# Attention feeding a gated MLP: the second stage begins two steps earlier, three weight pieces are converted beside it, and five smaller edits

## The chip, the cores and the metric

One NeuronCore of a Trainium2 chip runs the whole program. The metric is the device time of one execution in microseconds; smaller is better. The kernel before took 519.78 us (median of three runs, 519.24 to 522.22).

## What is computed

Float32 attention over 4 batches, 8 heads, 576 positions and head size 64, with rotary positions on q and k, feeds a small MLP with a convolution over positions in its gate. Cut to what matters:

```python
q_rot, k_rot = (rotate(q), rotate(k))
scores = 1.0 / np.sqrt(D) * np.matmul(q_rot, k_rot.transpose(0, 1, 3, 2))
attn = softmax(scores)                                # rows of 576
x = np.matmul(attn, v)  -> (B, S, H * D)              # 4 x 576 x 512
h = np.maximum(x @ w_in, 0.0)                         # 512 -> 1024
conv_out = sum over k of conv_w[k] * hp[:, k:k + S, :]    # 3 taps along S
out = h * sigmoid(conv_out) @ w_out                   # 1024 -> 512
```

`w_in`, `conv_w` and `w_out` arrive as 64-bit floats and are turned into 32-bit ones on the chip.

## The kernel before

**Pairs and steps.** Two heads make a pair, so there are 16 pairs (`p`), four to a batch. Each pair takes five steps (`s` 0 to 4): four of 128 queries for each of its two heads, and a last one with the 64 remaining queries of both. Step n = 5p + s. The order of all work is written by hand: `at(n, rank, fn)` puts a piece of work into step n, a smaller rank earlier, and every engine executes its own share in the order in which it was issued. `defer(k, fn)` puts work k ticks later, where a tick passes with about every group of products on TensorE.

**Attention of a step.** S (`emit_S`, line 245) makes the scores, VectorE takes the negated row maximum (`soft`, line 260), ScalarE the exponential with its row sum (line 264). T (`emit_T`, line 305) turns the probabilities on TensorE in 64-wide pieces, and ScalarE copies them into `pt` (line 189). The remainder turns (`emit_Trem`, line 333) do the last 64 keys; their copy is ScalarE's in the first stage and VectorE's (line 191) in the second. E (`emit_E`, line 362) multiplies the turned probabilities by v, once for each half (290 positions) of the sequence; `emit_rinv` sends the reciprocal sums through DRAM, and `norm` (line 380) and `split` (line 384) divide and store the result as a high and a low part in `xT`, the low part by GpSimd (line 387).

**Before the products.** The queue of SyncE loads q and k of a pair in 32-wide blocks; GpSimd rotates them (`rope`, lines 180 and 183), VectorE turns them in 32 x 32 blocks (`emit_TQ`, lines 224 and 228), and five ticks later ScalarE multiplies the turned q by the scale in place (line 225). `krem` (line 232) is a block-diagonal copy of the last 64 keys of both heads, used in the first stage.

**Two stages.** Up to step `WIDE` = 26 ("wide") only attention runs, with score tiles of three PSUM banks; S is issued a step ahead, and one product with `krem` (line 276) serves the last keys of both heads before the two wide ones (lines 280, 281). Beside it all 16 weight pieces (128 x 512, `conv_w_piece`, line 538) are converted: ScalarE line 497, VectorE lines 500, 506, 509 and 514, ScalarE line 557, GpSimd line 560 four times. From step 26 on ("narrow") the score tiles have two banks and two buffers, S is issued in its own step (a tile for each head, one tile for the last queries, made by four products of 64 x 64, lines 299 and 300), and the MLP runs between the attention products.

**The MLP.** Block `blk` is half a batch (288 positions). M1 (`emit_M1`, line 391) is 12 products for one of 8 feature groups; ScalarE takes the ReLU (409), then follow `conv` (VectorE, 413 and 415 twice, 2 ticks later), `tanh` (ScalarE, 421, 5 ticks), `gate` (VectorE, 424, 7 ticks) and `split` (ScalarE 432 and GpSimd 433, 9 ticks). M2 (`emit_M2`, line 469) is six products, a quarter of a 128-position tile of the output. Six blocks are spread over ten steps each from step `WIDE` on, by the weights `room` (line 666): 0.35 for a step with n % 5 of 0 or 1, which hold the E products (line 653), and 1.0 for the others. The last two blocks follow in a tail without attention.

## Time and profile before

| | |
|---|---|
| median of three runs | 519.78 us |
| the profiled execution's own time | 519.74 us |
| its span, first to last instruction | 518.0 us |
| busy: TensorE (PE) | 477.5 us, 92% of the span |
| busy: VectorE (DVE), ScalarE (ACT), GpSimd (POOL) | 370.4, 318.8, 300.4 us |
| mean granted TensorE clock | 0.974 of full speed |

The span and the execution's own time differ by 1.74 us, which lies around the span. TensorE is an in-order engine here: where it is busy all the time, work added to it or taken from it changes the time one for one, and where it waits, the engine it waits for decides. A window row gives its stretch, its length, the busy time (and instructions) of PE, of PE's weight loads, of DVE, ACT and POOL, then PEclk, the share of DMA and GB/s. "busy" of a stretch is read beside the length of the stretch; PEclk is the mean granted clock of that stretch, where 1.00 stands for 2.4 GHz and 0.50 for 1.2 GHz. In the rows `x8` counts instructions, and a float32 product is two of them. A bracket at the end of a row is the idle time before the instruction and what ended it.

### The profile page before, as it was taken

To read this page: it belongs to the slowest core of one execution; us is meant where nothing else is said; L and a number is where in the kernel's file an instruction comes from. 1 tells how busy PE (TensorE), PEld (TensorE's weight loads), DVE (VectorE), ACT (ScalarE), POOL (GpSimd) and SP (SyncE) were. 2 spreads that over 40 slices of the span, in tenths; PEclk is the share of its full clock that TensorE was granted. 3 is DMA by queue.
4 is the path that set the end of the run, shared out by engine and by line. 5 is a ranking of instruction groups with operands and counts; after the bars stand their busy time and mean duration, and the time that the engine had idled before them with its cause. 6 is when DMAs were issued, how large, how long until landed. Compare 5 with 4: busy or idle time off the path is not lost.

```text
span 518.0 us, 10786 instructions
## 1 busy us (share of the span) xinstructions
PE 477.5 (92%) x3880; PEld 350.1 (68%) x3880; DVE 370.4 (72%) x656; ACT 318.8 (62%) x836; POOL 300.4 (58%) x479
## 2 busy tenths in 40 slices
PE   2779789897999899999999999999999998999997
PEld 1346455563777477776867677767767676889986
DVE  5788988996597758694877578674867464748951
ACT  2678778886677566666666666674575554325520
POOL 3799978999585827665574838390482121314530
PEclk9979987997999899999999999999999999999999
DMA  8986664943424243434333341513320201000011
GB/s 225 174 165 152 160 145 137 212 98 69 93 47 93 48 91 68 93 68 92 68 73 66 87 74 44 105 52 83 59 67 1 66 2 45 21 22 22 0 42 61
DMA packets 139257, 42.61 MB, mean 82 GB/s; under 512 B 132012, under 2 KB 132804, under 8 KB 139204
## 3 DMA queue, kind: packets, MB, share of 16 engines
q1 hardware_dynamic: 137860, 41.54, 36.2%
q8 instruction: 30, 0.49, 0.4%
q10 hardware_dynamic: 1344, 0.39, 0.3%
q14 instruction: 23, 0.19, 0.1%
HBM read 37.12 MB, written 4.79 MB: 81 GB/s over the span
## 4 chain that ended last, share of the span: by engine, by line
PE 71%; DVE 10%; ACT 8%; SPq 3%; DMA 3%; issue 2%; POOL 2%; DVEq 0%; ACTq 0%; POOLq 0%
PE pm L401 13%; PE sp L252 13%; PE tp L368 13%; PE pm L479 11%; PE mt L479 8%; PE tp L312 6%; PE mt L401 5%; DVE negm L260 3%; ACT st L264 3%; ACT pt L189 3%; SPq L140 1%; DVE c L415 1%; PE sp L368 1%; DMA rq<-q 1%; DVE wt L506 1%
## 5 line engine op out<-in xcount | busy, mean ns | idle before, releaser
L260 DVE TENSOR_REDUCE negm<-sp 128x1 f32<-128x576 f32 x144 | 102.4, 747 | 57.2 <-PE sp L252 55.1
L189 ACT ACTIVATE pt<-tp 128x512 f32<-128x512 f32 (+3 forms) x176 | 84.3, 527 | 60.0 <-PE tp L312 59.6
L433 POOL TENSOR_TENSOR g<-c,g 128x288 fp32r<-128x288 f32 (+4 forms) x88 | 53.9, 625 | 91.0 <-ACT g L432 89.2
L252 PE MATMUL sp<-kT,qT 64*128 64x288 f32 (+4 forms) x556 | 105.0, 477 | 1.8 <-ACT str L264 1.0
L264 ACT ACTIVATE st<-sp,negm 128x576 f32<-128x576 f32 x128 | 93.8, 745 | 13.8 <-DVE negm L260 9.8
L415 DVE SCALAR_TENSOR_TENSOR c<-rr,cw,c 128x288 f32<-128x288 f32 x128 | 87.9, 686 | 4.5
L401 PE MATMUL pm<-xT,winh 128*128 128x290 f32 x384 | 83.3, 310 | 0.7 <-ACT rr L409 0.4
L387 POOL TENSOR_TENSOR xT<-xn,xT 128x290 fp32r<-128x290 f32 x32 | 28.9, 918 | 93.4 <-ACT xT L386 93.4
L252 PEld LDWEIGHTS sp<-kT,qT 64*128 64x128 f32 (+1 forms) x556 | 46.7, 177 | 33.6 <-issue 16.3
L401 PEld LDWEIGHTS pm<-xT,winh 128*128 128x128 f32 x384 | 61.1, 189 | 7.6 <-ACT rr L409 4.6
L479 PE MATMUL pm<-wouth,g 128*128 128x512 f32 x176 | 64.9, 410 | 0.0
L180 POOL TENSOR_TENSOR rq<-rq,tabt 128x192 f32<-128x192 f32 x90 | 60.0, 699 | 5.4 <-DMA rq<-q 5.4
L312 PEld LDWEIGHTS tp<-idf,st 64*128 64x128 f32 x1024 | 41.6, 139 | 27.2 <-ACT st L264 16.3
L368 PE MATMUL tp<-pt,vm 128*64 128x290 f32 x384 | 55.4, 433 | 4.8 <-ACT pt L189 4.8
L312 PE MATMUL tp<-idf,st 64*128 64x64 f32 x1024 | 47.9, 227 | 10.6 <-ACT st L264 10.5
L401 PE MATMUL pm<-xT,winl 128*128 128x290 f32 x192 | 56.8, 296 | 0.0
L180 POOL TENSOR_TENSOR rk<-rk,tabt 128x192 f32<-128x192 f32 x90 | 55.5, 650 | 0.0
L424 DVE SCALAR_TENSOR_TENSOR c<-c,rr 128x288 f32<-128x288 f32 x64 | 35.2, 554 | 15.7 <-ACT c L421 15.4
L368 PEld LDWEIGHTS tp<-pt,vm 128*64 128x64 f32 x384 | 26.7, 144 | 26.8 <-ACT pt L189 8.6
L413 DVE TENSOR_SCALAR c<-rr,cw 128x288 f32<-128x288 f32 x64 | 30.0, 468 | 15.9 <-ACT rr L409 15.9
L479 PEld LDWEIGHTS pm<-wouth,g 128*128 128x128 f32 x176 | 33.1, 188 | 7.2
L421 ACT ACTIVATE c<-c 128x288 f32<-128x288 f32 x64 | 28.4, 444 | 13.7 <-DVE c L415 13.3
(103 smaller groups left out, 811.7 us busy)
## 6 DMA issues: line engine op xcount, KB each, us to landing
out<-ot SPq DMA_DIRECT2D x17, 256.0 KB
rq<-q SPq DMA_DIRECT2D x30, 144.0 KB
rq<-q SPq DMA_DIRECT2D x60, 72.0 KB
rk<-k SPq DMA_DIRECT2D x30, 144.0 KB
rk<-k SPq DMA_DIRECT2D x60, 72.0 KB
w<-moe_w_in SPq DMA_DIRECT2D x8, 512.0 KB
vm<-v SPq DMA_DIRECT2D x32, 128.0 KB
w<-moe_w_out SPq DMA_DIRECT2D x8, 512.0 KB
```

Of the source, the lines that this page charges most:

```text
L180: nc.gpsimd.tensor_tensor(out=y, in0=y, in1=tabt[:, a:a + 3], op=ALU.mult)
L189: nc.scalar.activation(out=out, in_=in_, func=AF.Copy, scale=1.0 if sc is None else sc)
L252: nc.tensor.matmul(out=out, lhsT=qt[64 * h:64 * h + 64, c], rhs=kt[64 * h:64 * h + 64, a:a + n], start=True, stop=True)
L260: reds.setdefault((p, s), []).append(lambda: nc.vector.tensor_reduce(out=nm, in_=sc, axis=AX.XY if len(sc.shape) == 3 else AX.X, op=ALU.ma ...
L264: lambda: nc.scalar.activation(out=dst, in_=sc, func=AF.Exp, bias=nm, scale=1.0, accum_out=sm)
L312: nc.tensor.transpose(ps[r][:, 64 * k:64 * k + 64], x[i], idf[i, i])
L368: nc.tensor.matmul(out=xp[64 * h:64 * h + 64, :], lhsT=vmain[p][:, h, i, :] if i < 4 else vrem[:, h, :], rhs=pt[:, 2 * i + h if i < 4 else ...
L401: nc.tensor.matmul(out=ps[:, 0:XW], lhsT=w[:, kk, fs], rhs=xT[:, xs, e, :], start=(i == 0), stop=(i == n - 1))
L415: nc.vector.scalar_tensor_tensor(out=c, in0=r[:, j + e:j + e + HS], scalar=cw[:, 8 * e + f:8 * e + f + 1], in1=c, op0=ALU.mult, op1=ALU.add,)
L424: nc.vector.scalar_tensor_tensor(out=c, in0=c, scalar=1.0, in1=r[:, j + 1:j + 1 + HS], op0=ALU.add, op1=ALU.mult)
L433: nc.gpsimd.tensor_tensor(out=lo, in0=c[:, o:o + n], in1=hi.bitcast(F32), op=ALU.subtract)
L479: nc.tensor.matmul(out=ops[tt][:, 0:width], lhsT=g_tile(tt, f, e), rhs=w[:, f, cols], start=(f == 0 and i == 0), stop=(f == NF - 1 and i = ...
```

## The change

- `WIDE` is 24. Thirteen weight pieces are converted in the first stage (39 conversion steps over 23 steps, before 48 over 25). The last three, all of `w_out`, are converted in steps 26 to 32, in buffers of one each, the next piece's load being issued when the last one's third conversion step is.
- The root of the scale goes into both rotation tables, and the multiplication of the turned q (line 225) goes.
- In the first stage the `krem` product is issued after the two wide ones.
- In the second stage the last queries of both heads are laid out block-diagonally in `qrem` (two 64 x 64 VectorE transposes for each pair), and S of the last step is two full products in place of four quarter ones.
- In the second stage the copy of the remainder turns is ScalarE's.
- In blocks 0 and 1 the first tap is computed by ScalarE right behind the ReLU.
- Both E products of a pair are in step 5p + 5, and `room` is 0.5 for steps with n % 5 = 0 and 1.0 for all others.

```diff
-            defer(5, lambda: evac("A", QT[p], QT[p], scale))
+            if p * STEPS + 4 >= WIDE:
+                for h in range(2):
+                    r = slice(64 * h, 64 * h + 64)
+                    nc.vector.transpose(out=qrem[p % 2][r, r].rearrange("p (c i) -> p c i", i=32), in_=x[r, 16:18])
...
+                mm(ps[:, 0:512], 0, 64, 512, c)
+                mm(ps[:, 1024:1536], 1, 64, 512, c)
                 nc.tensor.matmul(
                     out=ps[:, 512:1024].rearrange("p (g n) -> p g n", g=8)[:, 0:8:7, :],
                     lhsT=qt[:, c], rhs=krem[p % 2], start=True, stop=True,
                 )
-                mm(ps[:, 0:512], 0, 64, 512, c)
-                mm(ps[:, 1024:1536], 1, 64, 512, c)
...
-            for h, j in ((0, 0), (1, 1), (0, 1), (1, 0)):
-                mm(ps[64 * h:64 * h + 64, j, 0:HS], h, HS * j + 64, HS, c)
+            for j in range(2):
+                nc.tensor.matmul(
+                    out=ps[:, j, 0:HS], lhsT=qrem[p % 2], rhs=kt[:, HS * j + 64:HS * j + 64 + HS],
+                    start=True, stop=True,
+                )
...
-        after(lambda: evac("V", pt[:, 8, 128 * first:128 * (first + num)], ps))
+        after(lambda: evac("A", pt[:, 8, 128 * first:128 * (first + num)], ps))
...
+        if blk < 2:
+            nc.scalar.activation(out=c, in_=r[:, j:j + HS], func=AF.Copy, scale=cw[:, f:f + 1])
...
-            nc.vector.tensor_scalar(out=c, in0=r[:, j:j + HS], scalar1=cw[:, f:f + 1], scalar2=None, op0=ALU.mult)
+            if blk > 1:
+                nc.vector.tensor_scalar(out=c, in0=r[:, j:j + HS], scalar1=cw[:, f:f + 1], scalar2=None, op0=ALU.mult)
...
+    WIDE = 24
+    NWIDE = 13
...
-    WIDE = 26
...
-                        at(n + 5 + i, 4 if n + 5 + i < WIDE else 10, lambda p=p, i=i: emit_E(p, i))
+                        m = n + 5 + (i if n + 5 < WIDE else 0)
+                        at(m, 4 if m < WIDE else 10, lambda p=p, i=i: emit_E(p, i))
...
+            for k, u in zip((4, 5, 6, 9, 10, 11, 14, 15, 16), sum(wcv[NWIDE:], [])):
+                at(WIDE + k // 2, 3 if k % 2 else 0.4, u)
...
-                room = [0.35 if n % STEPS < 2 and n < STEPS * NP + 2 else 1.0 for n in range(n0, n0 + MB)]
+                room = [0.5 if n % STEPS == 0 and n < STEPS * NP + 2 else 1.0 for n in range(n0, n0 + MB)]
...
+                    late["wb"] = (1, 1, 1)
+                    late["ws"] = ctx.enter_context(tc.tile_pool(name="ws2", bufs=1))
+                    load_w(NWIDE)
...
+    root = float(D) ** -0.25
+    cs = [(root * np.cos(fr)).astype(np.float32), (root * np.sin(fr)).astype(np.float32)]
```

## Rows read from the trace of the kernel before

**Rows 1.** Windows: wide steps to 23, steps 24 and 25, steps 26 to 35, 36 to 45.

```profile
16.00:116.80 100.80, 85.57 (x836) 52.30 (x832) 90.21 (x144) 82.56 (x210) 92.88 (x144) 0.92 0.70 155
116.80:128.40 11.60, 8.52 (x57) 4.07 (x55) 7.62 (x16) 7.34 (x21) 11.60 (x22) 0.71 0.41 77
128.40:179.70 51.30, 46.59 (x416) 33.60 (x414) 39.11 (x70) 35.81 (x91) 36.16 (x64) 0.97 0.35 71
179.70:234.80 55.10, 54.54 (x464) 40.51 (x462) 40.38 (x72) 36.60 (x93) 32.21 (x48) 1.00 0.35 75
```

**Rows 2.** Chain that ended last, narrow steps 46 and 47: start, length, what.

```profile
238.10 2.59 PE tp L368 x20
240.69 1.17 PE sp L252 x8
...
242.36 1.81 PE pm L401 x12
```

**Rows 3.** Chain, wide stage from 16 to 117 us: its shares, and one scale multiplication.

```profile
by line: DVE negm L260 14.6%; PE sp L252 8.6%; PE sp L368 6.4%; ACT st L264 6.2%; issue 6.1%; DVE wt L506 4.2%; DMA vm<-v 4.1%; POOL rq L180 3.9%; DVE wt L500 3.8%; DVE wt L509 3.6%; DMA vr<-v 3.3%; DMA rq<-q 3.1%; POOL woutl L560 3.1%; SPq
...
30.24 0.58 ACT qT L189
```

**Rows 4.** TensorE in order of time, steps 24 and 25.

```profile
116.84 0.46 PE L312 MATMUL tp<-idf,st 64*128 64x64 f32 x8
...
119.85 0.46 PE L276 MATMUL sp<-kr,qT 128*128 128x128 f32 x2 [1.81 <-DVE kr L232]
...
124.12 3.83 PE L368 MATMUL tp<-pt,vm 128*64 128x290 f32 x16 [0.53 <-ACT pt L189]
...
128.37 1.24 PE L252 MATMUL sp<-kT,qT 64*128 64x288 f32 x8
```

**Rows 5.** Groups by line, VectorE's conversions from 16 to 117.5 us.

```profile
L509 DVE SCALAR_TENSOR_TENSOR wt<-w,wt 128x512 int32<-128x512 int32 x15 | 13.8, 919 | 0.5
L514 DVE SCALAR_TENSOR_TENSOR wf<-w,wt 128x512 int32<-128x512 int32 x15 | 13.1, 873 | 0.4
L506 DVE TENSOR_SCALAR wt<-wt 128x512 int32<-128x512 int32 (+1 forms) x17 | 10.8, 632 | 0.6
L500 DVE TENSOR_SCALAR wt<-wt 128x512 f32<-128x512 f32 (+1 forms) x17 | 10.5, 620 | 2.9 <-ACT wt L497 2.8
```

**Rows 6.** GpSimd in order of time, about step 24.

```profile
116.85 6.49 POOL L560 TENSOR_TENSOR woutl<-wf,wouth 128x128 fp32r<-128x128 f32 x12
123.30 1.01 POOL L387 TENSOR_TENSOR xT<-xn,xT 128x290 fp32r<-128x290 f32 x1
```

**Rows 7.** TensorE in order of time, narrow steps 34 and 35; then the window after.

```profile
170.83 0.44 PE L337 MATMUL tp<-idf,st 128*128 128x128 f32 x2 [0.68 <-ACT pt L189]
...
172.92 0.99 PE L252 MATMUL sp<-kT,qT 64*128 64x288 f32 x5 [0.97 <-ACT str L264]
...
174.54 0.52 PE L312 MATMUL tp<-idf,str 64*128 64x64 f32 x9 [0.38 <-DVE pt L191]
175.53 3.72 PE L368 MATMUL tp<-pt,vm 128*64 128x290 f32 x16 [0.47 <-ACT pt L189]
...
176.00:178.00 2.00, 2.00 (x10) 0.94 (x8) 1.80 (x5) 1.55 (x4) 2.00 (x4) 0.50 0.00 0
```

**Rows 8.** TensorE in order of time, S of narrow steps 32 and 33.

```profile
158.32 1.24 PE L252 MATMUL sp<-kT,qT 64*128 64x288 f32 x8
162.51 1.71 PE L252 MATMUL sp<-kT,qT 64*128 64x288 f32 x7 [0.42 <-ACT st L264]
```

**Rows 9.** TensorE in order of time, S of narrow step 45.

```profile
229.69 1.47 PE L252 MATMUL sp<-kT,qT 64*128 64x288 f32 x7
...
231.00 0.40 PE L252 MATMUL sp<-kT,qT 64*128 64x288 f32 x1
```

**Rows 10.** TensorE, the four quarter products of a last step.

```profile
252.51 1.19 PE L252 MATMUL sp<-kT,qT 64*64 64x288 f32 x8
```

**Rows 11.** Groups by line and form: a ScalarE operation of a tap's size.

```profile
L421 ACT ACTIVATE c<-c 128x288 f32<-128x288 f32 x64 | 28.4, 444 | 13.7 <-DVE c L415 13.3
```

More of the change, by code (lines that the diff above doesn't have):

```diff
@@ L59, in attention_moe_kernel @@
     rvc = [keep.tile([128, 32], F32, name=f"rvc_{s}") for s in range(2)]
+    qrem = [keep.tile([128, 128], F32, name=f"qr_{s}") for s in range(2)]
     cw = keep.tile([128, 32], F32, name="cw")
@@ L493, in to_f32 @@
         h, l = w32[:, :, 1], w32[:, :, 0]
-        t = pool.tile([128, n], I32, tag="wt", name="wt", bufs=3)[0:w64.shape[0]]
+        t = pool.tile([128, n], I32, tag="wt", name="wt", bufs=late["wb"][1])[0:w64.shape[0]]
+        if w is None:
+            w = t.bitcast(F32)
         def first():
@@ L516, in third @@
             )
-        return first, clamp, second, third
+        return first, clamp, second, third, w
     def bits(i):
@@ L530, in load_w @@
     def load_w(i):
-        if i >= len(WPIECES):
+        if i >= len(WPIECES) or (i >= NWIDE) != ("m" in psum):
             return
         src, _, _, kk, c = WPIECES[i]
-        t = late["ws"].tile([128, 512], I64, tag="w64", name="w64", bufs=4)
+        t = late["ws"].tile([128, 512], I64, tag="w64", name="w64", bufs=late["wb"][0])
         nc.sync.dma_start(out=t, in_=src[kk * 128:kk * 128 + 128, c:c + 512])
@@ L542, in first @@
         def first():
-            box["w"] = late["ws"].tile([128, 512], F32, tag="wf", name="wf", bufs=3)
-            box["s"] = to_f32(late["ws"], stage.pop(i), box["w"], 512)
+            w = late["ws"].tile([128, 512], F32, tag="wf", name="wf", bufs=3) if i < NWIDE else None
+            box["s"] = to_f32(late["ws"], stage.pop(i), w, 512)
+            box["w"] = box["s"][4]
             box["s"][0]()
@@ L574, in conv_cw @@
         w = late["ws"].tile([32, 128], F32, tag="cwf", name="cwf", bufs=1)
-        for fn in to_f32(late["ws"], t, w, 128):
+        for fn in to_f32(late["ws"], t, w, 128)[:4]:
             fn()
@@ L606, in emit @@
             load0()
-            for x in rvc + krem + [x[:, S:S + 64] for x in strem]:
+            for x in rvc + krem + qrem + [x[:, S:S + 64] for x in strem]:
                 nc.vector.memset(x, 0.0)
```

15 lines of the change are left out of this document (6 added, 9 removed).

## The prediction

> **What bounds the kernel now.** I read first the busy time by windows, then the chain of waits, then single steps in order of time. In the narrow stage TensorE is full: 54.54 of 55.10 us in steps 36 to 45 [rows 1], and the chain there goes from one group of products to the next without a gap [rows 2]. Whatever TensorE does there counts one for one. In the wide stage it is not full: GpSimd is busy for 92.88 of 100.80 us, VectorE for 90.21, ScalarE for 82.56, TensorE for 85.57 at a mean clock of 0.92 [rows 1]. The chain changes hands all the time, and the largest share is VectorE's row maximum with 14.6% [rows 3]. So wide steps are paid at the pace of the helpers, narrow ones at that of TensorE. Two stretches fit neither: steps 24 and 25 take 11.60 us at a clock of 0.71, and the first ten narrow steps leave 4.7 of 51.30 us idle [rows 1].
>
> **Two steps leave the wide stage.** From the first turn of step 24 to the first S of step 26 TensorE's order takes 128.37 - 116.84 = 11.5 us [rows 4]. The same work in the narrow stage is S and T twice, from 240.69 to 242.36 or 1.67 us each, and one E at 2.59 us [rows 2]: 5.9 us. The MLP has the same number of products as before. Gain 5.6 us; the 1.81 us wait for the turned k in that stretch goes with it, since the first S of pair 5 is now issued a step later. What the new last wide step may lose in its turn is priced under the first M1.
>
> **Relief in the wide stage.** By step 24 VectorE has converted 15 pieces and half of the last; now it does 13, 2.4 fewer. A piece costs it 919 + 873 + 632 + 620 = 3044 ns [rows 5], so 7.3 us of work leave it. Not all was on the path: the three lines of the chain with a share (4.2, 3.8, 3.6%) and GpSimd's 3.1% are 14.7% of 101 us, 14.8 us for 15 pieces [rows 3], about 1.0 us each; 2.4 pieces give 2.4 us. The scale multiplication stood on the chain with 0.58 us [rows 3], and once more like it: 1.2 us. The turned `krem` keys are now needed after the two wide products and not before; this can save part of such a wait in the pairs before, 1.2 us as an estimate for three pairs from the 1.81 us of [rows 4] (a delay is excluded by the maximum needing all three products either way). Together 4.8 us, between 0 and 7.3 plus the small ones.
>
> **Starved narrow steps.** A step's S needs score tiles that the exponentials of the step before must free. Where MLP products fill the step this is hidden; where none stand there, TensorE waits. I laid the units out by `room` for both kernels. Before, steps 34 and 35 have none, and TensorE waited 0.68, 0.97, 0.38 and 0.47 us, then E ran from 175.53 to the end of that stretch at 179.70, 4.17 us in place of 2.59, at a granted clock of 0.50 [rows 1, 2, 7]: 4.1 us. Steps 45, 55, 65 and 75 have none either, but hold an E: there S took from 229.69 to 231.40, 1.71 against 1.17 us [rows 2, 9], and E directly behind T waits 0.47 as in [rows 7], 1.0 us each, 4.0 us. These 8.1 us go: E has an M2 unit ahead of it in steps 35, 40, 45 and on. In their place the new layout leaves steps 33, 43, 53 and 63 with S and T alone, 1.67 us of products. The attention's own pace from S to S is 4.19 us where it decides [rows 8], which would leave 2.5 us idle; in that step the scale multiplication, now gone, stood ahead of the exponential. I take 2.0 us each, 8.0 us, between 0.5 (what S lost in step 45) and 4.1 (steps 34 and 35 with their clock). E directly behind T remains in steps 25, 30 and 70: 3 x 0.47 = 1.4 us [rows 7]. Steps with a single M1 unit in block 0: four between two-tile S (26, 27, 31, 32) where two were (27, 32). Such a step took 4.19 us, and the S after it was late by 0.5 us more (seven instructions in 1.71 us, eight in 1.24 [rows 8]), against 3.7 us of products (1.67 + 1.81 [rows 2] and an estimated 0.2 for remainder turns): 1.0 us lost, 2.0 us for two more. Sum: 8.0 + 1.4 + 2.0 - 8.1 = 3.3 us lost.
>
> **Three pieces beside the MLP.** VectorE gets 9.1 us [rows 5] and loses eight first taps in block 0; ScalarE gets them, 0.44 us each as another operation of that size [rows 11], six operations on pieces (an estimate of 0.65 us each from the same row, for 512 columns against 288) and the remainder copies, and loses the scale. VectorE goes from 39.1 to about 44 and ScalarE from 35.8 to about 43 of 51 us [rows 1]. That covers them; but both issue in order, and a conversion ahead of a row maximum delays the next S. With buffers of one each, ScalarE's first operation on the next piece waits for GpSimd's last on the one before, with exponentials queued behind it; and the load on SyncE's queue waits for VectorE, with the loads of q and k and the reciprocals behind it. Those are needed three steps later or more, so I price the queue at 0. For the rest 1.0 us, between 0 and 4. In blocks 0 and 1 the maximum comes sooner by a tap; I count that in this term.
>
> **The first M1 and the clock.** M1 of block 0 now stands in step 24, and its last three products need the low part of pair 3, which GpSimd wrote at 123.30 behind twelve conversions [rows 6]. Eight of these are gone from there, and the low part would end at 116.85 + 6.49/3 + 1.01 = 120.0 us if GpSimd came no sooner; with step 24 at 116.84 less the relief, M1 asks for it about 3 us later (1.67 us of S and T, nine products). I price 1.5 us for this and for a lower clock behind the thin step 23, between 0 and 4.
>
> **At nothing.** Block-diagonal queries: four quarter products take 1.19 us [rows 10], two pairs at once, since eight 64-row instructions take as much (1.17 [rows 2]); two full ones take the same column time, estimate 0, bounds 0.5 us either way in all; their two transposes hide in VectorE's slack. The remainder copies on ScalarE end sooner than behind VectorE's taps. E twice in a step is the same work.
>
> **Sum.** -5.6 - 4.8 + 3.3 + 1.0 + 1.5 = -4.6 us: span 513.4, own time 519.74 - 4.6 = **515.1 us**; the profiled run lies at the median. About 0.5% (2.6 us) is what can be told from no change.
>
> **Rivals.** (a) *VectorE sets the wide stage*: the relief is 7.3 + 2.4 = 9.7 us in place of 4.8, and the first M1 and the pieces cost nothing (2.5 us): 515.1 - 4.9 - 2.5 = 507.7 us. For it, VectorE is 90% busy; against it, GpSimd is busier. (b) *GpSimd sets it*: it must still do five rotations and 13 pieces before M1 can use pair 3, and had done 12 pieces at 116.85 [rows 6]. Then the relief is 0 and the time 515.1 + 4.8 = 519.9 us, 518 to 521 with the small terms. (c) *Slower*: the empty steps 33, 43, 53 and 63 cost what 34 and 35 did, 4.1 us each with the clock at 0.50 behind them [rows 7]: 4 x 2.1 = 8.4 us more, 523.5 us. It decides as soon as more than two of the four show a lower granted clock. The Trainium skill, "TensorE: Matmul & The Clock Gate", section "A second HAM failure mode: psum-queue depth-cycling", says that short idle gaps between groups of matmuls while PSUM buffers cycle make the clock swing and cost throughput; by that rule this rival would be the likeliest and the sum 523.5. The trace agrees at step 35 alone, while the wait of 0.42 us in [rows 8] and the late S of [rows 9] were followed by no such fall: steps 36 to 45 have a clock of 1.00 [rows 1]. (d) That the MLP does not really begin at step 24 is contained in (b).
>
> **Chances.** Forecast 0.40 (its own range 511 to 519), (a) 0.22, (b) 0.18, (c) 0.20. The range 506 to 525 takes in (a) and (c) with some play; what is left out is a gain or a loss in which several bounds meet. Faster by over 0.5% (under 517.2): most of the forecast's lower part, 0.29, and (a), 0.51 in all; same: 0.28; slower: 0.21.
>
> **What would show it.** Right: the wide stage ends near 112 us and the first M1 begins within 5 us of that; steps 33, 43, 53, 63 show about 2 us of idle TensorE before S, released by the exponential; no scale multiplication; the middle blocks take 55 to 57 us. Wrong: a wide stage that ends at 117 us or later, a clock of 0.5 behind each empty step, or a first block above 55 us with VectorE or ScalarE full.

## The result and the profile after

The kernel after takes 527.22 us, median of four runs (524.93 to 527.71), against 519.51 us of the kernel before beside it: a ratio of 1.0119, 95% interval 1.0092 to 1.0147. It is 1.2% slower. The forecast was 515.1 us; its range ended at 525.0. Executions of one kernel below differ by up to 2.2%, so a ratio is taken over those within 1.5% of its kernel's fastest and a median over all; the profiled executions of fill and b24 lie outside that 1.5%. The profiled execution took 527.71 us with a span of 525.8 us, and 8.0 us lie between it and the profiled one of before.

Busy times on the page of the kernel after:

```profile
PE 475.5 (90%) x3834; PEld 355.0 (68%) x3834; DVE 352.8 (67%) x643; ACT 325.5 (62%) x859; POOL 298.9 (57%) x479
```

TensorE is busy for 2.0 us less than before (477.5), in a span 7.8 us longer: the new time is idle time of TensorE, and partly a lower clock (mean 0.961, before 0.974). Windows of the kernel after: wide steps to the last one's first turn, the rest of step 23, then, cut at starts of S, steps 24 and 25, 26 to 33, 34 to 43, 44 to 53 (columns as in [rows 1]):

```profile
16.00:112.45 96.45, 79.57 (x794) 48.01 (x795) 83.70 (x140) 74.26 (x192) 88.17 (x139) 0.91 0.66 142
112.45:117.65 5.20, 4.24 (x37) 3.19 (x37) 2.37 (x5) 4.49 (x14) 4.33 (x10) 0.55 0.41 69
117.65:129.85 12.20, 11.63 (x93) 7.57 (x91) 5.00 (x9) 6.89 (x18) 10.49 (x25) 0.91 0.54 116
129.85:173.41 43.56, 37.49 (x315) 27.24 (x313) 35.91 (x62) 34.96 (x87) 27.03 (x42) 0.96 0.42 93
173.41:230.25 56.84, 54.62 (x452) 41.81 (x452) 34.72 (x65) 41.09 (x105) 32.61 (x49) 0.97 0.34 71
230.25:285.98 55.73, 53.26 (x453) 40.82 (x453) 38.08 (x73) 37.39 (x102) 34.80 (x55) 1.00 0.36 76
```

The first S of step 24 starts at 117.65 us. Before, the work of step 24 began at 116.84 us [rows 4], so the work up to step 24 did not end sooner, although it holds VectorE's work for 2.4 pieces less. The groups by line confirm that this work is gone (VectorE's conversions of the kernel after, from 16 to 117.65 us; out<-in, count, busy us, mean ns, idle before):

```profile
L522 DVE SCALAR_TENSOR_TENSOR wt<-w,wt 128x512 int32<-128x512 int32 x13 | 11.7, 900 | 0.4
L527 DVE SCALAR_TENSOR_TENSOR wf<-w,wt 128x512 int32<-128x512 int32 x13 | 10.8, 832 | 0.3
L519 DVE TENSOR_SCALAR wt<-wt 128x512 int32<-128x512 int32 (+1 forms) x14 | 8.8, 626 | 0.5
L513 DVE TENSOR_SCALAR wt<-wt 128x512 f32<-128x512 f32 (+1 forms) x14 | 7.7, 551 | 2.2 <-ACT wt L510 2.1
```

That is 39.0 us against 48.2 us in [rows 5]: 9.2 us less, of which the 2.4 pieces are 7.3 and shorter means of the same operations the rest. S of step 23 is the last one that both kernels issue at the same place of their order. It and S of step 24 on TensorE, before (two rows) and after (one; the next S is at 117.65 below):

```profile
109.12 0.49 PE L276 MATMUL sp<-kr,qT 128*128 128x128 f32 x2
114.07 1.19 PE L252 MATMUL sp<-kT,qT 64*64 64x512 f32 x8
...
107.66 1.08 PE L256 MATMUL sp<-kT,qT 64*128 64x512 f32 x4
```

Up to S of step 23 the kernel after is 1.46 us ahead. From there to S of step 24 it takes 9.99 us, before 4.95. The end of the stage in order of time, on TensorE:

```profile
112.45 0.46 PE L319 MATMUL tp<-idf,st 64*128 64x64 f32 x8 [1.80 <-ACT st L268]
...
115.04 2.20 PE L375 MATMUL tp<-pt,vm 128*64 128x145 f32 x16
117.02 0.70 PE L375 MATMUL tp<-pt,vr 128*64 128x145 f32 x4
117.65 2.29 PE L304 MATMUL sp<-kT,qr 128*128 128x288 f32 x4
...
120.51 0.53 PE L408 MATMUL pm<-xT,winh 128*128 128x290 f32 x2
```

The last wide step has no S of a next step to run ahead. T waits 1.80 us for the exponential, the clock is 0.55 behind it, and S of step 24 takes 2.29 us where another takes 1.13 to 1.33. The first M1 itself waits for nothing. In the narrow stage a group of waits is there that the kernel before hardly has (waits of TensorE for an exponential before S: us in total, times, longest; before, then after):

```profile
PE sp L252 <- ACT st L264: 0.8, 2, 0.4
PE sp L304 <- ACT st L268: 10.0, 5, 2.9
```

The second row is S of the last queries, late behind the empty steps 33, 43, 53, 63 and, with 0.63 us, 73. Two of them on the timeline:

```profile
173.41 1.33 PE L304 MATMUL sp<-kT,qr 128*128 128x288 f32 x4 [1.84 <-ACT st L268]
...
343.60 1.24 PE L304 MATMUL sp<-kT,qr 128*128 128x288 f32 x4 [2.87 <-ACT st L268]
```

and the windows behind the four, of which three show what [rows 7] showed behind step 35:

```profile
176.00:178.00 2.00, 2.00 (x6) 1.57 (x7) 0.36 (x1) 1.63 (x4) 1.02 (x2) 0.54 1.00 165
231.00:233.00 2.00, 2.00 (x23) 1.41 (x22) 1.42 (x3) 1.62 (x4) 1.51 (x2) 1.00 0.66 130
288.00:290.00 2.00, 2.00 (x10) 1.59 (x7) 0.49 (x2) 1.68 (x4) 1.16 (x2) 0.50 1.02 190
345.00:347.00 2.00, 2.00 (x19) 1.64 (x16) 1.11 (x2) 1.58 (x4) 1.78 (x2) 0.52 0.34 74
```

### The profile page after: what moved, and what is told of

The parts are those of the page before. It is cut to its first block, busy times and chain, and to the rows that moved or that the text cites. A ratio compares the mean times of both kernels' runs of the same rounds, so it can differ in the third digit from the quotient of the medians.

```text
span 525.8 us, 10723 instructions
## 1 busy us (share of the span) xinstructions
PE 475.5 (90%) x3834; PEld 355.0 (68%) x3834; DVE 352.8 (67%) x643; ACT 325.5 (62%) x859; POOL 298.9 (57%) x479
## 4 chain that ended last, share of the span: by engine, by line
PE 65%; DVE 12%; ACT 10%; SPq 5%; DMA 4%; issue 3%; POOL 1%; DVEq 0%; ACTq 0%; POOLq 0%
PE tp L375 12%; PE pm L489 12%; PE pm L408 12%; PE sp L256 9%; PE mt L489 6%; PE tp L319 5%; PE mt L408 5%; ACT st L268 4%; DVE negm L264 3%; ACT pt L190 3%; PE sp L304 2%; SPq L141 2%; DVE c L425 1%; DMA w<-moe_w_out 1%; SPq L142 1%
## 5 line engine op out<-in xcount | busy, mean ns | idle before, releaser
L443 POOL TENSOR_TENSOR g<-c,g 128x288 fp32r<-128x288 f32 (+4 forms) x88 | 58.2, 674 | 151.3 <-ACT g L442 150.1
L190 ACT ACTIVATE pt<-tp 128x512 f32<-128x512 f32 (+3 forms) x200 | 93.4, 509 | 46.2 <-PE tp L319 42.6
L256 PE MATMUL sp<-kT,qT 64*128 64x288 f32 (+2 forms) x464 | 90.6, 488 | 2.8 <-ACT str L268 0.8
L425 DVE SCALAR_TENSOR_TENSOR c<-rr,cw,c 128x288 f32<-128x288 f32 x128 | 83.2, 651 | 9.2 <-ACT c L419 5.2
L489 PE MATMUL pm<-wouth,g 128*128 128x512 f32 x176 | 68.1, 428 | 0.0
L319 PE MATMUL tp<-idf,st 64*128 64x64 f32 x1024 | 49.8, 232 | 14.7 <-ACT st L268 13.5
L256 PEld LDWEIGHTS sp<-kT,qT 64*128 64x128 f32 (+1 forms) x464 | 41.3, 189 | 27.3 <-issue 9.7
L375 PE MATMUL tp<-pt,vm 128*64 128x290 f32 (+1 forms) x400 | 55.1, 420 | 2.7 <-ACT pt L190 2.7
L375 PEld LDWEIGHTS tp<-pt,vm 128*64 128x64 f32 x400 | 28.6, 142 | 24.4 <-ACT pt L190 3.7
L423 DVE TENSOR_SCALAR c<-rr,cw 128x288 f32<-128x288 f32 x48 | 19.9, 415 | 25.5 <-ACT rr L416 25.5
```

What stands on the lines that cost most here:

```text
L190: nc.scalar.activation(out=out, in_=in_, func=AF.Copy, scale=1.0 if sc is None else sc)
L256: nc.tensor.matmul(out=out, lhsT=qt[64 * h:64 * h + 64, c], rhs=kt[64 * h:64 * h + 64, a:a + n], start=True, stop=True)
L319: nc.tensor.transpose(ps[r][:, 64 * k:64 * k + 64], x[i], idf[i, i])
L375: nc.tensor.matmul(out=xp[64 * h:64 * h + 64, :], lhsT=vmain[p][:, h, i, :] if i < 4 else vrem[:, h, :], rhs=pt[:, 2 * i + h if i < 4 else ...
L425: nc.vector.scalar_tensor_tensor(out=c, in0=r[:, j + e:j + e + HS], scalar=cw[:, 8 * e + f:8 * e + f + 1], in1=c, op0=ALU.mult, op1=ALU.add,)
L443: nc.gpsimd.tensor_tensor(out=lo, in0=c[:, o:o + n], in1=hi.bitcast(F32), op=ALU.subtract)
```

## Experiments

Each kernel below is the kernel after with the edit shown; only "b24" starts from the kernel before. The table has the ratio to the kernel before, which ran beside it, and two times of the profiled execution: where the narrow stage's first S starts (step 24 or 26), and from there to the end of the last product. Second-stage times compare only among kernels with the same first narrow step. Differences of ratios are turned into us with 519.8.

| run | median us | ratio [95%] | narrow from | rest |
|---|---|---|---|---|
| before | 519.8 | 1 | 128.37 | 386.4 |
| after (24, 13 pieces) | 527.2 | 1.0119 [1.0092, 1.0147] | 117.65 | 405.0 |
| fill | 521.0 | 0.9994 [0.9962, 1.0026] | 122.29 | 397.4 |
| nw16 | 526.1 | 1.0126 [1.0096, 1.0156] | 126.11 | 398.3 |
| onvec | 535.0 | 1.0289 [1.0265, 1.0314] | 120.42 | 410.6 |
| w24n12 | 511.3 | 0.9824 [0.9794, 0.9854] | 111.66 | 396.0 |
| noclamp | 510.2 | 0.9816 [0.9779, 0.9854] | 111.48 | 395.3 |
| clamp2 | 520.0 | 0.9994 [0.9972, 1.0017] | 118.15 | 395.7 |
| low2 | 512.3 | 0.9843 [0.9818, 0.9869] | 110.83 | 396.3 |
| shift13 | 516.1 | 0.9906 [0.9869, 0.9943] | 116.50 | 396.3 |
| shift12 | 513.2 | 0.9865 [0.9833, 0.9897] | 112.64 | 395.7 |
| b24 | 526.9 | 1.0020 [0.9973, 1.0068] | 122.99 | 401.1 |
| **w26** | **507.7** | 0.9763 [0.9738, 0.9788] | 118.86 | 383.9 |
| w26n16 | 515.9 | 0.9912 [0.9880, 0.9943] | 128.47 | 382.4 |
| w26n12 | 510.0 | 0.9806 [0.9767, 0.9844] | 120.27 | 385.0 |
| w26old | 512.8 | 0.9854 [0.9813, 0.9895] | 119.48 | 390.7 |
| w26vec | 515.6 | 0.9902 [0.9877, 0.9927] | 118.61 | 390.2 |
| w26mul | 511.4 | 0.9808 [0.9753, 0.9864] | 122.05 | 385.4 |
| w26f | 512.1 | 0.9839 [0.9802, 0.9876] | 119.77 | 389.4 |
| pieces | 522.9 | 0.9993 [0.9955, 1.0030] | 125.92 | 391.9 |

"Narrow from" scatters between executions: fill runs the same first stage as the kernel after, and its profiled execution shows 122.29 where that one shows 117.65. The column is one execution of each kernel, and a difference of a few us in it is not a verdict by itself; the last section shows a cause.

### The empty steps, the pieces, VectorE and the start

**fill**

```diff
-                us = [(0.09 + 0.1 * f, lambda blk=blk, f=f: emit_M1(blk, f)) for f in range(NF)]
+                us = [(0.09 + 0.12 * f, lambda blk=blk, f=f: emit_M1(blk, f)) for f in range(NF)]
```

> All of the changed kernel, but the M1 units of a block stand at 0.09 + 0.12 f in place of 0.09 + 0.1 f of the block's room: one M1 each in steps 28, 29, 31, 32, 33 (and 10, 20 ... later) where 28 had two and 33, 43, 53, 63 and 73/83 had none; the steps with E keep their units. Theory 'empty steps' (the time is lost in the steps 33, 43, 53, 63 that hold S and T alone, by a wait of 1.8 to 2.9 us before the last-query S and by lower clocks behind it): the waits before S of steps 34, 44, 54, 64 fall under 0.7 us and 8 to 11 us go, 516 to 519 us. Theory 'pieces' (single-buffered weight pieces and more ScalarE work beside block 0): only block 0 is late, 1 to 2 us go, 525 us. Theory 'stage end' (the lost time is the serial last wide step and a wide stage that does not end sooner): no change, 527 us.

A gain of 6.5 us (1.0119 to 0.9994), and 7.6 us in the second stage (405.0 to 397.4): less than the 8 to 11 us expected here, and near the 8.0 us that the forecast gave for the four empty steps. The row of fill for that S (waits of TensorE) has no long wait left:

```profile
PE sp L304 <- ACT st L268: 5.4, 7, 1.1
```

**nw16**

```diff
-    NWIDE = 13
+    NWIDE = 16
```

> All of the changed kernel, but all 16 weight pieces are converted in the first stage again (48 conversion steps over 23 steps), none beside the MLP. Theory 'pieces': block 0 (steps 24 to 33, 55.8 us, against 51.3 us for the first block of the kernel before) gains 3 to 4.5 us and the time is 523 us. Theory 'relief has no worth' (the last wide steps are serial, with fewer pieces or not): step 24 begins at 117.65 us plus at most 1. Theory of the prediction (1.0 us for a piece in the first stage, 1.0 us for all three beside the MLP): step 24 begins 3 us later and block 0 gains 1.0 us: 529 us. Theory 'empty steps': block 0 gains less than 1.5 us, blocks 1 to 4 do not change.

The time is the same within the intervals. But the two stages moved against each other: the first is 8.5 us longer, the second 6.7 us shorter. Steps 24 to 33 of nw16, beside 55.76 us (117.65 to 173.41) of the kernel after:

```profile
126.11:176.54 50.43, 46.74 (x405) 34.16 (x403) 32.90 (x58) 38.48 (x99) 31.86 (x58) 0.99 0.39 78
```

So three pieces cost 5.3 us in these ten steps, not 1.0; and in the first stage 2.8 us each, not 1.0. Both prices were too low, and the theories that put the loss on one of them fall; so does that of the empty steps alone, which gave the pieces less than 1.5 us.

**onvec**

```diff
-        if blk < 2:
+        if blk < 0:
...
-            if blk > 1:
+            if blk >= 0:
...
-        after(lambda: evac("A", pt[:, 8, 128 * first:128 * (first + num)], ps))
+        after(lambda: evac("V", pt[:, 8, 128 * first:128 * (first + num)], ps))
```

> All of the changed kernel, but the copy of the remainder turns in both stages that went to ScalarE and the first taps of blocks 0 and 1 are VectorE's again (so the copy is VectorE's in the second stage as before; in the first stage it has always been the same function and goes to VectorE here as it did before). Theory 'ScalarE overloaded' (the last-query S waits for the exponential because ScalarE does more in front of it): the waits before that S fall from 1.8 to 2.9 us to about 1.0 us, and the time falls by 3 to 6 us. Theory 'empty steps': the waits stay within 0.5 us of what they are and the time within 2 us of 527; block 0 may lose up to 2 us since VectorE has the taps and the pieces.

8.8 us slower, against the theory that ScalarE was overloaded and outside the 2 us of the other. The second stage, which is all that the edit touches, is 5.6 us longer in the profiles (410.6 against 405.0): the taps and copies on ScalarE are worth that; the rest is the first stage's own scatter or not traced. Steps 24 to 33 take 58.13 us, VectorE is busy for 46.10 of them. S of step 30 waits 2.39 us, S of step 34 2.56 us (kernel after: 0.81 and 1.84).

**w26**

```diff
-    WIDE = 24
+    WIDE = 26
```

> All of the changed kernel, but the second stage begins at step 26 as before (13 pieces are spread over 25 steps, the other three stand in steps 28 to 34); the layout then leaves step 34 without a unit and steps 35, 45, 55, 65 with the two E products and nothing ahead of them. Theory 'beginning at 24 is worth it' (prediction: two steps leave the wide stage, 5.6 us): 5 us slower than the changed kernel but for what the layout changes. Theory 'stage end' (the last wide step is serial wherever it stands, and the start at 24 gains little): the time is within 2 us of the changed kernel or below it. Theory 'empty steps': no S waits 1.8 us or more except near step 34, blocks 1 to 4 take 55 to 56 us each, 520 to 523 us in all.

This run decides most. One number put back gives 18.5 us (1.0119 to 0.9763), and the kernel is 2.4% faster than before, a time that only the theory of the stage's end left room for. The number stands for three things, though: steps 24 and 25 are wide again, the 39 conversion steps are spread over 25 steps, and steps 33, 43, 53 and 63 are no longer empty (6.5 us by fill). The wide stage, then steps 26 to 35 and 36 to 45 of w26:

```profile
16.00:118.86 102.86, 85.98 (x891) 52.77 (x891) 91.80 (x150) 83.65 (x219) 98.35 (x157) 0.95 0.71 145
...
118.86:175.61 56.75, 50.62 (x427) 36.41 (x425) 41.73 (x74) 43.33 (x109) 39.34 (x69) 0.97 0.44 92
175.61:229.53 53.92, 53.45 (x454) 41.59 (x452) 36.23 (x64) 40.42 (x102) 32.26 (x50) 1.00 0.36 77
```

26 wide steps end 9.5 us sooner than before (128.37), and only 1.2 us later than 24 of them in the kernel after. Here the relief is there. Steps 26 to 35 are 5.4 us longer than before (51.30 in [rows 1]); the next run tells how much of that is the pieces'.

### What each part is worth with the start at 26

**w26n16**

```diff
-    WIDE = 24
-    NWIDE = 13
+    WIDE = 26
+    NWIDE = 16
```

> The changed kernel with the second stage at step 26 and all 16 weight pieces in the first stage (48 conversion steps over 25, as in the kernel before); the layout, the scale in the tables, the late krem product, the block-diagonal queries, the copies and the taps stay changed. Against the run with 13 pieces there and the stage at 26 (507.7 us, step 26 at 118.86 us). Theory 'pace' (the first stage is paid by conversion steps per attention step, 1.56 there, 1.70 with the stage at 24, 1.92 before): step 26 begins at 127 to 129 us, as in the kernel before (128.37), block 0 (steps 26 to 35, 56.75 us with the pieces) falls to about 52 us, 512 to 514 us in all. Theory 'small edits' (the scale and the krem order freed the first stage, not the pieces): step 26 begins at 119 to 121 us and the time is 503 to 506 us.

The theory of pace holds for the first stage: narrow from 128.47 us, before 128.37; the time is 2 us above what it gave. Against w26 the three pieces give 9.6 us in the first stage and cost 1.5 us in the second (383.9 against 382.4), 1.9 of it in steps 26 to 35 (54.83 and 56.75 us) before some comes back; 7.7 us in all by the ratios. The other 3.5 us of those ten steps are not the pieces'. With 16 pieces the new scale and the `krem` order do not move the end of the first stage in these two executions.

**w26n12** (`WIDE = 26`, `NWIDE = 12`, and three places more for the fourth piece)

```diff
-            for k, u in zip((4, 5, 6, 9, 10, 11, 14, 15, 16), sum(wcv[NWIDE:], [])):
+            for k, u in zip((4, 5, 6, 9, 10, 11, 14, 15, 16, 19, 20, 21), sum(wcv[NWIDE:], [])):
```

> As the run with the second stage at step 26, but 12 pieces in the first stage (36 conversion steps over 25) and four beside block 0 (steps 28 to 36). Theory 'pace': a piece less gives about 3 us in the first stage (9.5 us for three) and costs about 1.8 us in block 0 (5.4 us for three): 506 to 507 us. Theory 'a threshold' (with 13 pieces TensorE's clock already stays near 1.00 in the first stage, and more relief finds TensorE full): the first stage ends within 1 us of 118.86 and the time is 508 to 511 us.

2.2 us slower, intervals overlapping: no gain is left in a piece less, as the theory of a threshold had it.

**w26old**

```diff
-                        m = n + 5 + (i if n + 5 < WIDE else 0)
+                        m = n + 5 + i
...
-                room = [0.5 if n % STEPS == 0 and n < STEPS * NP + 2 else 1.0 for n in range(n0, n0 + MB)]
+                room = [0.35 if n % STEPS < 2 and n < STEPS * NP + 2 else 1.0 for n in range(n0, n0 + MB)]
```

> As the run with the second stage at step 26 and 13 pieces, but with the layout of the kernel before: the two E products of a pair in two steps and room 0.35 for both. Theory 'layout is neutral' (what was lost in steps 33, 43, 53, 63 came from the start at 24, which moves the same weights onto other steps): within 2 us of 507.7. Theory 'layout gains' (an M2 ahead of both E, and no thin steps): 3 to 6 us slower, the blocks from step 36 on at 55.1 us as in the kernel before, not 53.6 to 54.1.

4.7 us slower, 6.8 us in the second stage alone: started at 26, the new layout and the paired E are a gain.

**w26vec** (`WIDE = 26` with the edit of onvec)

> The changed kernel with its second stage at step 26, but the first taps of blocks 0 and 1 and the copies of the remainder turns are VectorE's. With the stage at 24 that cost 7.8 us (535.0 against 527.2), 3.7 of it in block 0 and 2.7 in block 1. Theory 'VectorE sets block 0 while the pieces are there': 511 to 514 us, block 0 longer by 3 to 4 us, later blocks within 0.5 us but for block 1. Theory 'it was the empty steps that made VectorE's delay count': within 2 us of 507.7.

7.2 us slower, of it 3.3 us in steps 26 to 35 (60.06 us) and 1.2 us in the next ten. Steps 26 to 35:

```profile
118.61:178.67 60.06, 51.98 (x426) 36.20 (x425) 46.50 (x86) 39.06 (x97) 42.80 (x75) 0.94 0.44 91
```

The 3.3 us stand behind the empty step 34. Up to its S w26vec is 1.6 us quicker than w26 (43.25 and 44.85 us from the first narrow S); from there to S of step 36 it takes 16.81 us, w26 11.90. S of step 35 and a window behind it, in w26vec, then that S in w26:

```profile
168.17 1.13 PE L256 MATMUL sp<-kT,qT 64*128 64x288 f32 x5 [2.28 <-ACT str L268]
...
172.00:174.00 2.00, 2.00 (x10) 0.95 (x8) 0.92 (x4) 1.65 (x5) 2.00 (x5) 0.50 0.01 1
...
167.13 1.83 PE L256 MATMUL sp<-kT,qT 64*128 64x288 f32 x7
```

So here too VectorE's load costs most where a step holds no unit.

**w26mul** (`WIDE = 26`, and three hunks of the change undone: the turned q is multiplied by the scale again, `krem` is issued first, four quarter products replace the block-diagonal ones)

> The changed kernel with its second stage at step 26, but the scale is multiplied into the turned q again, the krem product comes first and S of the last queries is four quarter products. Prediction's price: 2.4 us for the first two (1.2 each), 0 for the third: 510 us. Theory 'free' (with 16 pieces the first stage ended at 128.47 with these edits and 128.37 before without them): 506.5 to 509 us.

2.3 us slower, near what the first two were priced at (2.4), but the intervals overlap: not told from nothing.

**pieces** (as w26mul, with the edits of w26old and w26vec: what is left of the change is the three pieces)

> The kernel before with one part of the change alone: 13 weight pieces in its first stage and the last three beside the MLP (its second stage begins at step 26, its layout, its scale multiplication, its quarter products, its copies and taps stay). Prediction's price: relief 2.4 us and up to 1.0 us lost beside the MLP for these three pieces, 518 to 519 us. Theory 'pieces carry the gain' (8.1 us between 16 and 13 pieces with all other edits in): 511 to 513 us, the first stage ends near 119 us (128.37 before) and the first ten steps behind it take about 4 us longer than before's 51.3.

No change that can be told; a gain as priced (0.8 to 1.8 us) lies within the interval, the one of the other theory doesn't. The second stage pays 5.5 us for the three pieces (391.9 against 386.4) when VectorE keeps the taps and copies in the old layout, 1.5 us when ScalarE has them in the new one. By the ratios the parts are not a sum: pieces alone 0, pieces with all else 7.7. But the profiled first stage, 125.92 us against 118.86 in w26, holds one VectorE instruction of 7.46 us (last section), so that the pieces give nothing by themselves is not shown.

**b24** (the kernel before with `WIDE = 24`, and the condition of the remainder turns as in the change)

> The kernel before with the second stage at step 24 and nothing else (all 16 pieces in the first stage, 48 conversion steps over 23 in place of 25). Prediction's price: two steps leave the first stage, 5.6 us gained, less a starved layout: 514 to 518 us. Theory 'pace' (fewer steps carry the same conversions, and the last wide step has no S ahead): the first stage hardly ends sooner for its two steps less, step 24 begins at 124 us or later, and the time is 525 us or more, as the changed kernel with 16 pieces and the stage at 24 (526 us).

Between 0.3% faster and 0.7% slower: beginning at 24 alone gives nothing that can be told, and the 514 to 518 us expected from the forecast's price are excluded.

### Which engine sets the wide stage

**w24n12** (`NWIDE = 12` with the places of w26n12 and the M1 units of fill)

> The changed kernel (second stage at step 24) with 12 pieces in the first stage, 36 conversion steps over 23, and so the same 1.57 for a step as in the run with the stage at 26 and 13 pieces; four pieces beside block 0; M1 units spread so that no step is empty (as in the run 'fill', 521 us). Theory 'pace': the first stage runs as in the run at 26, step 24 (last-query S) begins at about 108 us in place of 117.65, and the time is 511 to 514 us. Theory 'narrow start' (what is lost by beginning at 24 is lost at the change of stage: the last wide step without an S to run ahead, the clock there, and steps 24 and 25 in narrow form): step 24 begins at 114 us or later and the time is 518 to 522 us.

8.8 us faster than fill, with a second stage as long (396.0, 397.4): one piece less in the first stage is worth 8.8 us there. The time is the one that the theory of pace gave (511 to 514 us); S of step 24 at 111.66 us lies between the two theories, since the serial last step is there too.

**noclamp** (from fill; the clamp of the first 13 pieces is left out, so values beyond the 32-bit range would not be limited)

```diff
-            box["s"][1]()
+            if i >= NWIDE:
+                box["s"][1]()
             box["s"][2]()
```

> The run 'fill' (second stage at 24, 13 pieces in the first stage, M1 units spread; 521.0 us) without the clamp of the 13 pieces of the first stage, so values outside the range of 32-bit floats are not limited there. VectorE does 13 x 0.62 = 8 us less in the first stage, GpSimd and ScalarE the same. Theory 'VectorE sets the first stage at 24': 6 to 9 us gained, 512 to 515 us, as with a piece less there (511.3). Theory 'GpSimd sets it' (its split of a piece and the rotations): under 2 us gained, 519 to 521 us.

**clamp2** (from w24n12)

```diff
             box["s"][1]()
+            if i < NWIDE:
+                box["s"][1]()
             box["s"][2]()
```

> The run with the second stage at 24 and 12 pieces in the first stage (511.3 us), with the clamp of each of these 12 done twice: VectorE does 12 x 0.62 = 7.4 us more there, two and a half pieces' worth of its work. Theory 'VectorE sets it': 7 to 9 us lost, 518 to 520 us. Theory 'GpSimd sets it': within 2 us of 511.3. Theory 'a threshold in the clock' (any engine's delay that starves TensorE for long lets the clock fall and the loss is then larger than the delay): 520 us or more with a first-stage clock under 0.90.

**low2** (from w24n12)

```diff
-                for o in range(0, 512, 128):
+                for o in (0, 0, 128, 256, 384) if i < NWIDE else (0, 128, 256, 384):
```

> The run with the second stage at 24 and 12 pieces in the first stage (511.3 us), with one of the four quarters of each piece's low part computed twice: GpSimd does 12 x 0.54 = 6.5 us more there, three pieces' worth of its work. Theory 'GpSimd sets it': 6 to 9 us lost, 517 to 520 us. Theory 'VectorE sets it': within 2 us of 511.3.

The three agree. Without 8 us of VectorE's work the kernel gains 9.3 us; 7.4 us more of it cost 8.8; 6.5 us more on GpSimd cost 1.0, inside the interval. With the start at 24 and these places of the conversions VectorE sets the pace of the wide stage, at about 1.2 us for each us. The window of the wide stage up to S of step 24, in noclamp:

```profile
16.00:111.48 95.48, 80.26 (x832) 49.73 (x831) 78.31 (x131) 78.56 (x205) 89.51 (x145) 0.95 0.70 148
```

the same in clamp2:

```profile
16.00:118.15 102.15, 79.92 (x831) 49.44 (x831) 92.93 (x152) 77.41 (x203) 91.45 (x144) 0.95 0.61 133
```

and in low2:

```profile
16.00:110.83 94.83, 81.04 (x832) 50.04 (x831) 82.85 (x140) 77.42 (x203) 93.59 (x151) 0.95 0.66 142
```

The clock is 0.95 in all three, so it is not the clock that tells them apart. For what each is compared with, that holds of w24n12 but not of fill (the same window of fill, then of w24n12):

```profile
16.00:122.29 106.29, 86.79 (x831) 53.35 (x830) 89.72 (x144) 78.74 (x205) 90.44 (x148) 0.88 0.62 132
16.00:111.66 95.66, 79.54 (x831) 49.26 (x831) 85.87 (x140) 77.32 (x203) 90.25 (x144) 0.94 0.67 141
```

So clamp2 against w24n12 shows VectorE's price with the clock left out: 6.5 us in this window at 0.95 and 0.94. In the gain of noclamp, and in the 8.8 us between fill and w24n12, the clock has a part, and so may have one clamp that lasts 4.99 us in fill (last section): the same products kept TensorE busy for 86.79 us in fill, 80.26 in noclamp, 79.54 in w24n12. GpSimd is busy for a larger share than VectorE in noclamp and low2 (94 and 99%, VectorE 82 and 87%) and yet doesn't decide; as I read it, because the row maximum stands between a score and the next one and most of GpSimd's work does not. It is not out of it either: up to S of step 23 of the kernel after, VectorE's turn of q waits for GpSimd's rotation twice, 2.5 us in all.

More GpSimd work was tried only with 12 pieces, and neither ScalarE's work nor the loads of the weights were varied: up to S of step 23 ScalarE waited once for a piece of `w_in`, 0.6 us in the kernel after, 2.9 in shift13, 3.8 in nw16, never in w26 and w24n12.

**shift13, shift12** (from fill and from w24n12; 20 and 18 in the two)

```diff
-                at((WIDE - 1) * i // len(wsteps), 0.4, u)
+                at(((WIDE - 1) * i + 20) // len(wsteps), 0.4, u)
```

> The run 'fill' (second stage at 24, 13 pieces in the first stage, 521.0 us) with the same 39 conversion steps put half a step later on the scale of attention steps: 20 of the 39 stand a step later than they did, and none leaves the first stage. Theory 'load' (VectorE's work in the first stage sets the pace, wherever it stands): within 2 us of 521. Theory 'place' (which attention steps get two conversion steps, beside the turned k and the normalization, decides): a change of 4 us or more, in either direction, since 13 pieces cost 9 us more than 12 while VectorE's work for one, 3.0 us, accounts for 3.6 by the doubled clamp's 1.2 us for each us.

> The run with the second stage at 24 and 12 pieces in the first stage (511.3 us), its 36 conversion steps shifted in the same way. Theory 'load': within 2 us of 511.3. Theory 'place': a change of 4 us or more, most likely slower, 515 to 521 us.

With nothing but the places of the conversion steps changed, 13 pieces become 4.6 us faster; 12 become 2.1 us slower, with intervals that overlap, which neither theory gave. A piece now costs 2.1 us (0.9906 against 0.9865, overlapping too), not 8.8. So most of the 8.8 us hung on the places; how much of it through the clock (0.93 up to S of step 24 in shift13, 0.88 in fill) is open. VectorE in order of time shows what a place is; kernel after, between the row maxima of steps 18 and 19:

```profile
91.23 1.41 DVE L264 TENSOR_REDUCE negm<-sp 128x1 f32<-128x576 f32 x2
92.56 0.45 DVE L513 TENSOR_SCALAR wt<-wt 128x512 f32<-128x512 f32 x1
93.04 0.56 DVE L519 TENSOR_SCALAR wt<-wt 128x512 int32<-128x512 int32 x1
93.64 0.82 DVE L522 SCALAR_TENSOR_TENSOR wt<-w,wt 128x512 int32<-128x512 int32 x1
94.38 0.76 DVE L232 STREAM_TRANSPOSE kT<-rk 128x576 f32<-128x576 f32 x1
...
95.72 0.62 DVE L389 TENSOR_TENSOR xn<-xn,rb 128x290 f32<-128x290 f32 x1
96.27 0.74 DVE L264 TENSOR_REDUCE negm<-sp 128x1 f32<-128x576 f32 x1
```

Conversions, the turned k and a normalization stand in one queue ahead of one row maximum. Which of the collisions cost most was not tried, and stays open.

**w26f** (`WIDE = 26`, M1 units at `0.09 + 0.115 * f`)

> The changed kernel with its second stage at step 26 and M1 units at 0.09 + 0.115 f: step 34 has a unit, steps 44, 54 and 64 have two, and the E products of steps 30, 40, 50 and 60 have none ahead of them. Theory 'empty steps': step 34 gains 1 to 1.5 us, four E directly behind T lose 0.5 us each: 507 to 509 us, against 507.7 without the spread.

A miss: 4.0 us slower. Steps 26 to 35 take 58.9 us (56.75 in w26), though only the places of M1 moved. TensorE's clock there, in w26f:

```profile
160.00:162.00 2.00, 2.00 (x12) 1.31 (x11) 0.86 (x2) 1.97 (x7) 0.41 (x1) 0.50 1.36 201
162.00:164.00 2.00, 2.00 (x18) 1.62 (x17) 2.00 (x4) 0.91 (x3) 0.00 (x0) 0.50 1.50 169
164.00:166.00 2.00, 2.00 (x10) 2.00 (x10) 1.97 (x7) 1.86 (x5) 0.00 (x0) 0.50 0.60 103
```

and in w26, where it is back sooner, and where the empty step 34 (from 163.71 us) has no lower clock behind it:

```profile
160.00:162.00 2.00, 2.00 (x20) 1.88 (x20) 1.97 (x5) 1.81 (x5) 0.00 (x0) 0.50 1.36 153
162.00:164.00 2.00, 2.00 (x12) 1.95 (x11) 2.00 (x7) 1.62 (x6) 0.00 (x0) 0.68 0.47 95
164.00:166.00 2.00, 1.49 (x20) 0.92 (x18) 1.93 (x4) 1.97 (x6) 0.69 (x1) 1.00 0.84 162
```

Filling an empty step is no rule, then: in w26 the step cost little, and in w26f E without an M2 ahead waits 0.52 us in step 40. What makes the clock fall for longer in w26f was not tried. w26 stays the best.

## Why the prediction was wrong

By the forecast's own sum -4.6 us, measured +8.0 us between the profiled executions. Cut at the first S of step 26: after 129.85, before 128.37, and one M1 (1.81 us) and one E (2.59 us) [rows 2] are done earlier in the kernel after, so the work up to there became 2.9 us cheaper and the rest 10.8 us dearer. The forecast had -8.9 (-5.6, -4.8, +1.5) and +4.3 (+3.3, +1.0). Each half missed by 6 to 6.5 us.

**"Relief in the wide stage" failed.** The work left VectorE as counted: 47 conversion steps are issued ahead of step 24 in the kernel before, 39 in the kernel after. But step 24 began 0.8 us later where 4.8 us earlier was forecast, and S of step 23, which the end of the stage does not touch yet, came 1.5 us sooner. What was wrong is the price by the mean, 1.0 us for a piece from shares of the chain. The runs show 2.8 to 3.2 us for each of three (nw16; w26n16 against w26), 8.8 for the thirteenth at step 24, 2.1 for it in other places, and nothing for the thirteenth at 26. There is no one price. Up to S of step 23 the kernel before has issued 45 conversion steps, the kernel after 39, w26 36; the first six, with the small edits, were worth 1.46 us, the last three 7.44 (107.66 to 100.22), although w26 differs from the kernel after up to there in little but their spread. The windows up to that S, kernel after and w26:

```profile
16.00:107.66 91.66, 76.58 (x767) 46.21 (x768) 79.02 (x132) 72.09 (x187) 83.38 (x132) 0.91 0.67 144
16.00:100.22 84.22, 71.25 (x766) 44.38 (x768) 78.02 (x127) 70.80 (x185) 79.71 (x127) 0.98 0.76 156
```

VectorE is busy for 1.0 us less in w26, TensorE for 5.3 us less with the same products, at 0.98 in place of 0.91. Late row maxima, the places of the conversions and the lower clock go together here, and no run tells what each is worth. Two steps less also took back part of what three pieces less had given: 1.92 conversion steps for each attention step before, 1.70 after, 1.56 in w26. Thirteen pieces took almost the same wide stage for 24 steps (117.65) as for 26 (118.86); w24n12, at 1.57, ended it 6 us sooner. The count is not the whole of it: shift13 has 1.70 as well and is 4.6 us faster than fill, and w26n12, at 1.44, ends the stage 1.4 us later than w26.

**"Two steps leave the wide stage" gave a third of its price.** Cut at S of step 24 it looks right: steps 24 and 25 took 12.20 us, less 4.40 for M1 and E 7.8 us, against 11.5 before; -3.7 us, forecast -4.1 with the 1.5 us priced under the first M1. But what the new last wide step loses belongs to that price, and lies ahead of this cut. From S of step 23 to S of step 26 it is 17.8 us without M1 and E, before 19.25: a gain of 1.5 us. The 11.5 us held the end of a wide stage, which the forecast took for saved; it moved along, and S of step 23 and the next S are now 9.99 us apart in place of 4.95. The comparison also set S twice against a stretch that holds it once, since S of step 24 had been issued ahead, at 114.07. The first M1 needed no wait; T's 1.80 us, the half clock (S at 2.29 us) and 0.47 us before E are what was lost.

**"Three pieces beside the MLP" failed by its size.** 1.0 us, between 0 and 4; nw16 shows 6.7 us in the second stage. It was right only for the kernel with the start at 26 (1.5 us). These 5.7 us are most of the 6.5 that the second half missed. The cover I named was VectorE's mean share, 44 of 51 us. Behind an empty step a late exponential goes straight into TensorE's wait (2.56 us in onvec, 2.28 in w26vec); that VectorE's queue makes it late is argued from the edit, not followed in the trace. The taps and copies on ScalarE are worth about 6 us of the second stage (5.6 in onvec, 6.3 in w26vec), where I counted them inside a term of 1.0.

**"Starved narrow steps" held.** 8.0 us for the four empty steps, 6.5 by the ratio of fill and 7.6 between the profiles; waits of 1.84, 2.22, 2.47 and 2.87 us where I took 2.0 each. E behind an M2 unit waits for nothing, as forecast; directly behind T it waits 0.47, 1.67 and 0.52 us in steps 25, 30 and 70, where I took 0.47 each. The old layout's cost, 8.1 us, is 4.7 by the ratio of w26old and 6.8 in its second stage, less what the new layout costs there itself.

**"At nothing"** held within what the runs can tell: scale, `krem` order and block-diagonal queries together 2.3 us with overlapping intervals; the first two were priced 2.4 under the relief.

**The rivals.** (a) had the right engine and the wrong time: VectorE does set the wide stage, and 9.6 us are to be had from it, but with the start at 26. (b), GpSimd, is refuted by low2 for 12 pieces; for 13, noclamp speaks against it, where less VectorE work gave 9.3 us. Its number was nearer than the forecast's. (c) is the one whose sign came: three of four empty steps had a lower clock behind them, its own condition, and the measured time is 3.7 us above its number; but its price, 16.4 us for the empty steps, is more than twice what filling them gave. The time comes near (c) only by luck, through the two other misses. The Trainium skill ("TensorE: Matmul & The Clock Gate", section "A second HAM failure mode: psum-queue depth-cycling") names the swing of the clock between bursts; the trace agrees in three of the four windows above (0.54, 0.50, 0.52), not at 231 to 233 us (1.00). The waits themselves sum to 9.4 us in the four steps.

## What to carry to other kernels

When side work is spread over the steps of a stage, count side work per step before making the stage shorter, and try other places for it: two steps less with the same thirteen pieces brought nothing, and the same steps with a better spread brought 4.6 us. A stretch that looks dear because a stage ends in it is not saved by ending the stage earlier; the end moves along. Price an edit on the engine that stands between one score and the next by loading and relieving that engine alone (a doubled operation is a cheap test); shares of the chain gave a third of it here. When several edits arrive together, undo the boldest one first: the others together were worth 12 us, and the start at 24 took away 18.5, its empty steps and denser conversions included; with those two mended (w24n12) all but 3.2 us were back.

## What was unexpected

By the ratios the parts do not add up. Three pieces beside the MLP are worth 7.7 us when ScalarE has the first taps, and nothing (0.9993) with the rest of the change undone. And the same first stage does not take the same time: up to S of step 23 the profiled execution of the kernel after takes 107.66 us, that of fill 112.23.

Most of these 4.57 us is one instruction. A clamp of a piece takes 0.40 to 1.03 us in the kernel after. One of them takes 4.99 us in fill, 4.97 in onvec, 2.21 in shift13 and 7.46 in pieces, and each ends 0.28 us behind the last of a row of GpSimd instructions that follow one another without a gap. The clamp and the end of that row, in fill, then in pieces:

```profile
89.05 4.99 DVE L513 TENSOR_SCALAR wt<-wt 128x512 f32<-128x512 f32 x1
92.05 1.70 POOL L574 TENSOR_TENSOR woutl<-wf,wouth 128x128 fp32r<-128x128 f32 x4
...
35.65 7.46 DVE L507 TENSOR_SCALAR wt<-wt 128x512 f32<-128x512 f32 x1
41.14 1.69 POOL L184 TENSOR_TENSOR rk<-rk 128x192 f32<-128x192 f32 x3
```

In the second stage five other VectorE instructions are held in the same way, for 2.7 to 3.8 us where such a one mostly takes 0.46 to 0.63 (three in b24, one each in w24n12 and w26f). GpSimd runs beside nearly every clamp of the kernel after and of w26 without this, so the overlap alone does not do it; what does, and in which of the other executions it happened, is open.
